# Attention and a gated FFN in one kernel: loads of w_out in pieces of 64 columns, two of its loads triggered sooner, and q and k of heads 8 to 17 prepared at other ticks

## The chip, the cores and the metric

The kernel runs on one core of one Trainium2 chip. The time is the device time of one launch in microseconds (us). A core has five engines: TensorE (PE, with its weight loads shown apart as PEld), VectorE (DVE), ScalarE (ACT), GpSimd (POOL) and SyncE (SP), which mostly issues DMAs. Transfers run on 16 DMA engines beside them. Three runs of the kernel before gave 1164.59, 1169.75 and 1159.92 us, so the median is 1164.59 us.

## The reference

```python
# attention: batch 8, heads 8, S = 576, head size 64
scores = q @ k.T / 8
cum  = cumsum(maximum(s, 0))                       # one s per position and head
bias = minimum(-(cum[:, None] - cum[None, :]), 0)
scores = where(causal, -1e9, scores + bias)
attn = exp(scores - max); attn = attn / (sum + 1e-9)
x = (attn @ v), heads side by side                 # 4608 rows x 512
# gated FFN, the weights are float64 in HBM
gate = 1 / (1 + exp(-(x @ w_gate)))                # w_gate, w_val: 512 x 1536
out  = (gate * (x @ w_val)) @ w_out                # w_out: 1536 x 512
```

q, k, v and s are float32, and so is the output.

## The kernel before, in words

**Heads and ticks.** There are 64 heads (8 batches of 8). Each has 5 query tiles, and the main loop counts a tick n for each tile of each head, n = 5*i + t for head i and tile step t. Heads go in pairs p = i // 2, with j = i % 2. Heads 0 to 7 run in float32 (functions that begin with n_; tiles such as s7, na_ps, nt_ps, nx_ps). From head 8 on, q and k are split into a high and a low float16 half, and the work is done in three float16 products.

**One head from 8 on.** load_qk (L338) fetches q and k of a pair; qk_square and qk_scale find a power of two to scale them by; split_qk (L378) makes the halves by two ACT copies (L386, L388) and two DVE operations (L387, L389) and issues one DMA transpose on SP's queue (L394), which writes two thirds of the tile T. swap_k (L398) then copies two halves of T into its last third by two SBUF-to-SBUF DMAs, also on SP's queue (L399, L400). T has two buffers. For each tile, s_part multiplies T with the first third (L445) and then with the last (L446), so the first product needs the transpose and the second needs the swap. max_part (L470, L473) adds the bias from the row rl (L454), takes the minimum and the exponential on DVE and ACT; p_part splits the probabilities (L477, L482) and transposes them by DMA on SP's queue (L493) into pt; av_part (L505 to L507) multiplies with v. load_crow (L405) brings the row of cumulated s of the next head into one of two buffers, again on SP's queue.

**Weights.** The three weights come as pairs of int32, are decoded on DVE (L271 to L273) and split into float16 high and low (L291 on ACT, L292 on DVE). There are 18 steps. Steps 0 to 11 take one block of 128 columns of w_gate and w_val each; steps 12 to 17 take 256 rows of w_out each, 1 MB in float64, by two DMAs of 512 KB on ACT's queue (L251 and L258). The room for raw weights is shared: `outroom` lists for each w_out step which raw buffer it uses, which one for decoding, and after which step its load may start. weight_step decodes one step and triggers the loads that its step sets free.

**FFN.** From tick 44 on, three FFN units per tick are put between the heads until the first two g are through: unit (g, f) takes 256 rows of x and one of 12 blocks of the hidden size. ffn_in (L656) gives the tile gv, ffn_mid the split hidden tile h, ffn_out (L686) the product of h with w2[f], 512 columns of w_out as the moving operand, into o. The first two g wait for their ffn_out until w_out is there.

**What sets the order.** A scheduler with a model of the engines' times picks, per engine, among the steps that the ticks have made ready; `first()` gives a block a high priority, and `pin` or keep_in_program_order holds an instruction at its place. A moved step can so move others on all engines. Each engine then carries out its list in order.

The lines that change most around the heads are:

```python
if j == 0 and t == 4 and i + 2 >= NN:   # NN = 8
    qk_square(p + 1)
if NN - 1 <= i and j == 1:
    if t == 0:
        qk_scale(p + 1)
    if t == 1:
        split_qk(i + 1)
if t == 3 and NN - 1 <= i:
    swap_k(i + 1)
```

Of the kernel before, what the change touches and what calls it, by code (L numbers as in the profile page):

```python
# [7 lines left out]
F16 = mybir.dt.float16  # L8
F32 = mybir.dt.float32
F32R = mybir.dt.float32r  # L10
I32 = mybir.dt.int32
# [5 lines left out]
P = 128  # L17
# [6 lines left out]
def tile_attention_then_gated_ffn(  # L24
# [13 lines left out]
    NT, DM = out.shape  # L38
    DFF = w_gate.shape[1]
    NH = B * H  # L40
    NPAIR = H // 2
    NC = DM // P
    NF = DFF // P
# [4 lines left out]
    NTL = len(TILES)  # L48
# [4 lines left out]
    NN = H  # L53
# [3 lines left out]
    cp = ctx.enter_context(tc.tile_pool(name="cp", bufs=1))  # L57
# [10 lines left out]


    w1 = [cp.tile([P, NC, 2, 2, P], F16, name=f"w1_{f}") for f in range(NF)]  # L70
    w2all = cp.tile([P, NF, 2, DM], F16, name="w2all")
    w2 = [w2all[:, f] for f in range(NF)]
    e_s = [cp.tile([P, n * P], F32, name=f"e_{i}") for i, (_, _, n) in enumerate(SETS)]
    p_s = [cp.tile([P, 2, n * P], F16, name=f"p16_{i}") for i, (_, _, n) in enumerate(SETS)]

# [128 lines left out]
    spare = {}  # L204
# [6 lines left out]

    raw0 = lp.tile([P, 8 * P, 2], I32, name="ws0")
    dec0 = lp.tile([P, 8 * P], I32, name="wa0")
    flat = w2all.rearrange("p f l n -> p (f l n)").bitcast(I32)
    raw = [raw0] + [flat[:, i * 16 * P : (i + 1) * 16 * P].rearrange("p (n t) -> p n t", t=2) for i in range(2)]
    dec = [dec0] + [flat[:, i * 8 * P : (i + 1) * 8 * P] for i in range(4, 6)]

# [3 lines left out]

    for i in (1, 2):
        raw.append(t2big[:, 8 * i * GT : 8 * (i + 1) * GT].bitcast(I32).rearrange("p (n t) -> p n t", t=2))
    outroom = [(4, 0, 0), (5, 0, 0), (0, 0, NF - 3), (3, 0, NF - 1), (0, 0, NF + 2), (0, 0, NF + 4)]

    def room(n):

# [6 lines left out]
    def load_weight(n):  # L234
        o, f = wsteps[n]
        fs = slice(f * P, (f + 1) * P)
        r, d, _ = room(n)
        for x, src in enumerate((w_out,) if o else (w_gate, w_val)):
            src = src[f * P : (f + 2) * P, :] if o else src[:, fs]
            if wide:  # L240
                src = src.bitcast(I32)
                dst = r.rearrange("p n t -> p (n t)")
            else:
                dst = d.bitcast(F32)
            if o == 0:
                src = src.rearrange("(c p) n -> p c n", p=P)
                dst = dst.rearrange("p (c x n) -> p c x n", c=NC, x=2)[:, :, x]
            else:
                src = src.rearrange("(x p) (h n) -> h p x n", p=P, h=2)
                dst = dst.rearrange("p (x h n) -> h p x n", x=2, h=2)  # L250
                ins = nc.scalar.dma_start(dst[0], src[0])  # L251
                if n < NF + 2:
                    tc.keep_in_program_order(ins)
                src, dst = src[1], dst[1]
            if n < 2:
                nc.sync.dma_start(dst, src)
            else:
                ins = nc.scalar.dma_start(dst, src)  # L258
                if n == 2 or NF <= n < NF + 2:
                    tc.keep_in_program_order(ins)  # L260

    def decode_weight(n):

        o, f = wsteps[n]
        r, a, _ = room(n)
        if not wide:
            return a.bitcast(F32)
        m = w2all[:, f : f + 2].rearrange("p f l n -> p (f l n)") if o else w1[f].rearrange("p c g l n -> p (c g l n)")
        m = m.bitcast(I32)
        nc.scalar.activation(a.bitcast(F32), r[:, :, 1].bitcast(F32), AF.Copy, scale=2.0 ** -112)  # L270
        nc.vector.tensor_scalar(m, a, 3, 0x7FFFFFF8, ALU.logical_shift_left, ALU.bitwise_and)  # L271
        nc.vector.scalar_tensor_tensor(a, a, -0x80000000, m, ALU.bitwise_and, ALU.bitwise_or)
        nc.vector.scalar_tensor_tensor(a, r[:, :, 0], 29, a, ALU.logical_shift_right, ALU.bitwise_or)  # L273
        return a.bitcast(F32)

    def split_weight(n, a):

        o, f = wsteps[n]
        if o:
            a = a.rearrange("p (x n) -> p x n", x=2)  # L280
            hi, lo = w2all[:, f : f + 2, 0], w2all[:, f : f + 2, 1]
        else:
            a = a.rearrange("p (c n) -> p c n", n=P)
            hi, lo = (w1[f].rearrange("p c g l n -> p (c g) l n")[:, :, l] for l in range(2))
        ss = wp.tile([P, 1], F32, tag="wss", name=f"wss{n}")
        nc.scalar.activation(hi, a, AF.Square, accum_out=ss)
        tot = wp.tile([P, 1], F32, tag="wst", name=f"wtot{n}")
        nc.gpsimd.partition_all_reduce(tot, ss, P, ADD_REDUCE)
        pow2_of(wscale[:, o, f : f + 1 + o], tot, f"w{n}")
        sc = wscale[:, o, f : f + 1]  # L290
        nc.scalar.activation(hi, a, AF.Copy, scale=sc)  # L291
        nc.vector.scalar_tensor_tensor(lo, a, sc, hi, ALU.mult, ALU.subtract)  # L292
# [43 lines left out]
    qk32, qkc, T, crow, v32, v16, vx, PT, xq, S_ps, rl, AV = {}, {}, {}, {}, {}, {}, {}, {}, {}, {}, {}, {}  # L336
# [14 lines left out]
    def qk_square(p):  # L351
        t = qk32[p]
        ss = ssq[p % 2]
        for i in range(2):
            junk = wp.tile([QP, 2 * QC * D], F16, tag="jq", name=f"jq{p}_{i}", bufs=1)
            pin(nc.scalar.activation(junk, t[:, i].rearrange("p h c d -> p (h c d)"), AF.Square,
                                     accum_out=ss[:QP, i : i + 1]))
        tot = wp.tile([P, 2], F32, tag="qkt", name=f"qkt{p}")
        nc.gpsimd.partition_all_reduce(tot, ss, P, ADD_REDUCE)
        qkc[p] = tot  # L360
# [353 lines left out]
    for wnext["load"] in range(2):  # L714
        load_weight(wnext["load"])
# [13 lines left out]
    for n in range(nticks + 12):  # L729
        if n == NTL * EARLY:  # L730
            more_room()
        i, t = divmod(n, NTL)
# [10 lines left out]
        if 2 <= n < nticks + 2:  # L743
            a, z = divmod(n - 2, NTL)
# [5 lines left out]
        if 1 <= n < nticks + 1:  # L750
            a, z = divmod(n - 1, NTL)
# [7 lines left out]
        if 3 <= n < 3 + NTL * NN:  # L759
            with first():  # L760
                a, z = divmod(n - 3, NTL)
# [11 lines left out]
        if i < NH:  # L773
            p, j = divmod(i, 2)
            b, h = divmod(i, H)
# [4 lines left out]
            if i + 2 < NN:  # L780
                if j == 0 and t == 1:
                    n_load(p + 1)
                    load_v(p + 1)
                if j == 1 and t == 2:
                    with first():
                        n_prep(p + 1)
            elif j == 0 and t == 2 and i + 2 < NH:
                if p + 1 not in qk32:
                    load_qk(p + 1)
                if i < NN:  # L790
                    load_v(p + 1)
            if NN <= i and i + 1 < NH and j == 1 and t == 2:
                load_v(p + 1)
            if NN <= i and j == 0 and t == 0:
                split_v(p)
            if not spare:
                if j == 0 and t == 4 and i + 2 >= NN:
                    qk_square(p + 1)
                if NN <= i and j == 0 and t == 1:
                    split_qk(i + 1)  # L800
                if NN - 1 <= i and j == 1:
                    if t == 0:
                        qk_scale(p + 1)
                    if t == 1:
                        split_qk(i + 1)
                if t == 3 and NN - 1 <= i:
                    swap_k(i + 1)
            elif i <= EARLY + 1:
                if j == 0:
# [46 lines left out]
            elif b == 1:  # L856
                if VSQ <= n < VSQ + vch:
                    v_square(2, n - VSQ)
                if VSQ + 5 <= n < VSQ + 5 + vch:
                    c = VSQ + 4 + vch - n  # L860
# [15 lines left out]
        if n >= NE and state["u"] < 2 * NF:  # L876
            fdone = min(NF, int((n - NE + 1) * FPT))
            while state["u"] < 2 * fdone:
                f = state["u"]
# [17 lines left out]
        m = n - (11 if n > 2 * NTL * H + 30 else 7)  # L897
# [40 lines left out]
```

## Time and profile before

| | |
|---|---|
| median of three runs | 1164.59 us |
| profiled execution, its own time | 1161.21 us |
| its span | 1159.4 us, 30337 instructions |
| granted TensorE clock, mean | 0.979 |
| busy in the span | PE 1095.0, DVE 775.0, ACT 749.2, POOL 264.9 us |
| DMA | 157.62 MB, mean 136 GB/s |

The profiled execution took 1.8 us more than its span. TensorE is busy for 94% of the span; the gaps lie in the first third. The page's slices are 29 us each. In the answers by window, each engine has its busy time and, in brackets, the number of its instructions; then come the granted clock as a share of full speed, the busy share of the DMA engines and the GB/s. In a timeline a row begins with the start and the duration in us, and brackets at its end hold the idle time before the instruction and what ended it. SPq and ACTq rows are the issues of DMAs. In the groups by line, the last numbers are busy us in all and mean ns of one instruction.

### The profile page before, as it was taken

How to read it: one execution, taken by the hardware profiler on the slowest of the kernel's cores; microseconds unless marked ns; L12 is line 12 of the kernel's file. 1: busy time of each engine (PE TensorE's matmuls, PEld its weight loads, DVE VectorE, ACT ScalarE, POOL GpSimd, SP SyncE). 2: the span in 40 equal slices, each digit the busy share in tenths (PEclk: the TensorE clock that was granted, in tenths of full speed). 3: DMA queues.
4: the chain of work that ended last, by engine and by line, in shares of the span. 5: the costliest groups of instructions: out<-in, count | busy, mean ns of one | idle time of the engine just before them, and what ended most of it. 6: DMA issues, size and time to landing. Idle time of an engine off the chain costs nothing.

```text
span 1159.4 us, 30337 instructions
## 1 busy us (share of the span) xinstructions
PE 1095.0 (94%) x11644; PEld 855.9 (74%) x11644; DVE 775.0 (67%) x2393; ACT 749.2 (65%) x1465; POOL 264.9 (23%) x570
## 2 busy tenths in 40 slices
PE   6786789989999999999999999999999999999997
PEld 5664677656777887778777777778877887787775
DVE  6888879785788777776566577777777775222221
ACT  6988667776777877676656577667777764233222
POOL 5535333231222222121111122222222221000000
PEclk9879899999999999999999999999999999999999
DMA  9675678898889797886737578877877764000000
GB/s 276 199 223 141 129 152 167 177 186 160 154 164 193 151 187 157 153 160 115 164 66 150 99 159 167 168 152 164 154 160 145 146 122 88 12 20 19 1 19 19
DMA packets 435886, 157.62 MB, mean 136 GB/s; under 512 B 403551, under 2 KB 423007, under 8 KB 435742
## 3 DMA queue, kind: packets, MB, share of 16 engines
q1 hardware_dynamic: 418398, 127.12, 57.1%
q10 hardware_dynamic: 13824, 16.78, 4.6%
q0 software_dynamic: 3520, 11.80, 3.1%
q8 instruction: 91, 1.49, 0.5%
q14 instruction: 53, 0.43, 0.1%
HBM read 56.92 MB, written 9.58 MB: 57 GB/s over the span
## 4 chain that ended last, share of the span: by engine, by line
PE 60%; issue 23%; DMA 5%; DVE 4%; ACT 3%; POOL 3%; SPq 1%; ACTq 0%; POOLq 0%; DVEq 0%
PE gv L656 33%; PE o L686 16%; PE s L446 3%; PE s L445 3%; DMA pt<-p 1%; PE av L505 1%; PE av L507 1%; PE av L506 1%; DMA T<-T 1%; POOL rl L460 1%; DMA T<-qk 1%; POOL cr L460 1%; PE na_ps L604 1%; DVE e L470 1%; DMA nqk<-in_q_dram 1%
## 5 line engine op out<-in xcount | busy, mean ns | idle before, releaser
L656 PE MATMUL gv<-x,w 128*128 128x256 f16 (+3 forms) x6912 | 614.9, 247 | 3.9 <-DVE t2f L663 2.3
L656 PEld LDWEIGHTS <-w 128*128 128x128 f16 x6912 | 535.1, 98 | 61.4 <-issue 4.6
L686 PE MATMUL o<-w2all,h 128*128 128x512 f16 x1296 | 314.8, 379 | 0.0
L460 POOL TENSOR_SCALAR_AFFINE_SELECT rl<-rl 128x64 f32<-128x64 f32 (+1 forms) x280 | 113.7, 407 | 512.0 <-DVE em L470 453.3
L473 ACT ACTIVATE e<-e,em 128x576 f32<-128x576 f32 x280 | 154.4, 554 | 88.0 <-DVE em L470 85.9
L661 ACT ACTIVATE th<-gv,scb 128x256 f32<-128x256 f32 (+3 forms) x288 | 111.3, 411 | 147.5 <-PE gv L656 142.5
L686 PEld LDWEIGHTS <-h 128*128 128x128 f16 x1296 | 123.4, 98 | 106.4
L663 DVE SCALAR_TENSOR_TENSOR t<-th,gv 128x256 f32<-128x256 f32 x192 | 80.0, 417 | 133.1 <-ACT th L661 131.9
L470 DVE CUSTOM_DVE_ANT_0 e<-s,rl,qkcf 128x288 f32<-128x288 f32 x280 | 135.7, 485 | 32.1 <-PE s L446 27.8
L671 ACT ACTIVATE h<-t,hsc 128x256 f16<-128x256 f32 x192 | 96.6, 503 | 80.4 <-DVE t L663 80.3
L482 DVE SCALAR_TENSOR_TENSOR p<-e,p 128x384 f16<-128x384 f32 x224 | 102.6, 498 | 41.0 <-ACT p L477 40.2
L672 DVE SCALAR_TENSOR_TENSOR h<-t,hsc,h 128x256 f16<-128x256 f32 x192 | 93.3, 486 | 43.4 <-ACT h L671 42.6
L477 ACT ACTIVATE p<-e 128x1152 f16<-128x1152 f32 x112 | 112.0, 1000 | 2.5
L505 PE MATMUL av<-v,pt 128*128 128x65 f16 x560 | 67.8, 193 | 5.3 <-DMA pt<-p 5.3
L446 PE MATMUL s<-T 128*128 128x288 f16 (+2 forms) x246 | 62.1, 279 | 11.3 <-DMA T<-T 11.3
L445 PE MATMUL s<-T 128*128 128x288 f16 (+2 forms) x246 | 64.4, 279 | 7.1 <-DMA T<-qk 4.2
L694 POOL DMA_DIRECT2D out_dram<-osb x36 | 20.4, 566 | 211.5 <-ACT osb L693 210.9
L507 PE MATMUL av<-v,pt 128*128 128x65 f16 x560 | 67.8, 194 | 0.0
L506 PE MATMUL av<-v,pt 128*128 128x64 f16 x560 | 67.7, 192 | 0.0
L505 PEld LDWEIGHTS <-pt 128*128 128x128 f16 x560 | 52.5, 98 | 11.0 <-DMA pt<-p 6.1
L408 POOL PARTITION_BROADCAST cr<-cr x63 | 58.5, 929 | 2.1 <-DMA cr<-cum_d 2.0
L506 PEld LDWEIGHTS <-pt 128*128 128x128 f16 x560 | 52.5, 97 | 4.9
(155 smaller groups left out, 1415.0 us busy)
## 6 DMA issues: line engine op xcount, KB each, us to landing
out_dram<-osb POOLq DMA_DIRECT2D x36, 256.0 KB, 2.8
v<-v SPq DMA_DIRECT2D x56, 162.5 KB
v<-in_v_dram SPq DMA_DIRECT2D x64, 128.0 KB
T<-T SPq DMA_DIRECT2D x82, 72.0 KB
t2f<-in_v_dram SPq DMA_DIRECT2D x20, 288.0 KB
qk<-in_q_dram SPq DMA_DIRECT2D x17, 288.0 KB
qk<-in_k_dram SPq DMA_DIRECT2D x17, 288.0 KB
w2all<-in_moe_w_gate_dram ACTq DMA_DIRECT2D x7, 512.0 KB
```

The costliest lines, as they stand in the source:

```text
L445: nc.tensor.matmul(ps[:, : b_ - a], lhs, T[i][:, 0, a:b_], start=True, stop=False)
L446: nc.tensor.matmul(ps[:, : b_ - a], lhs, T[i][:, 2, a:b_], start=False, stop=True)
L460: nc.gpsimd.affine_select(rl[i][:, q0:w], rl[i][:, q0:w], pattern=[[-1, m]], compare_op=ALU.is_ge, fill=-MASKED if i < NN else MASKED, bas ...
L470: nc.vector.tensor_tensor_reduce(e_t[t][:, a:b_], ps[:, : b_ - a], rl[i][:, a:b_], c, init, ALU.add, ALU.min, acc)
L473: nc.scalar.activation(e_t[t][:, :w], e_t[t][:, :w], AF.Exp, bias=init, scale=-1.0)
L477: nc.scalar.activation(p_s[h_][:, 0], e_s[h_], AF.Copy, scale=PSCALE)
L482: nc.vector.scalar_tensor_tensor(flat[:, LOW[t] * P : (LOW[t] + t) * P], e_t[t][:, : t * P], PSCALE, flat[:, kb * P : (kb + t) * P], ALU.m ...
L505: nc.tensor.matmul(AV[i][:, t], hi, v_[:, D : 2 * D + 1], start=kb == 0, stop=False)
L506: nc.tensor.matmul(AV[i][:, t, 0:D], hi, v_[:, 0:D], start=False, stop=False)
L656: nc.tensor.matmul(ps[:, gv, a:e], w1[f][:, cc, gv, wl], x_of(b, cc)[:, xl, c0 + a : c0 + e], start=(c == 0), stop=(c == 3 * NC - 1))
L661: nc.scalar.activation(th[:, a:e], ps[:, 0, a:e], AF.Tanh, scale=scb[b][:, f : f + 1])
L686: nc.tensor.matmul(ps[:m], h[:, hl, tt * P : tt * P + m], w2[f][:, wl], start=(f == 0 and c == 0), stop=(f == NF - 1 and c == 2))
```

## The change

**Layout of w_out.** w2all, the split w_out, was `[P, 12, 2, 512]` (block f, high or low, columns). It is now `[P, 6, 2, 8, 2, 64]`: a pair of blocks, high or low, eight groups of 64 columns, which block of the pair, and the 64 columns. The two halves of one block's row are no longer next to each other: w2[f] is eight runs of 64 columns with a gap of 64 between them. Each load of 512 KB was a half of the columns of 256 rows, in pieces of 256 columns (2 KB in float64); it is now 128 rows with all columns, in pieces of 64 columns (512 B). What split_weight writes, high and low, is now one run of 1024 each; before it was two runs of 512.

**Rooms.** The fifth w_out step (16) now uses the raw buffer of the second one (13) and has the mark `NF + 1`: its load is triggered in weight_step of step 14 (before: of step 15). The sixth (17) takes the room ws0 with the mark `NF + 2`: its load is triggered in step 15 (before: in step 17).

**Ticks.** In the part of the loop for heads 7 to 17, load_qk goes from t = 2 to t = 0 or 1, qk_square from t = 4 to t = 2 or 3, qk_scale from t = 0 of the next head to t = 3 or 4, split_qk from t = 1 to t = 0 (for head 8 to tick 34), and swap_k from t = 3 to t = 2 (for head 8 to tick 36).

```diff
--- before.py
+++ after.py
@@ -68,8 +68,9 @@
 
 
     w1 = [cp.tile([P, NC, 2, 2, P], F16, name=f"w1_{f}") for f in range(NF)]
-    w2all = cp.tile([P, NF, 2, DM], F16, name="w2all")
-    w2 = [w2all[:, f] for f in range(NF)]
+
+    w2all = cp.tile([P, NF // 2, 2, 8, 2, DM // 8], F16, name="w2all")
+    w2 = [w2all[:, f // 2, :, :, f % 2] for f in range(NF)]
     e_s = [cp.tile([P, n * P], F32, name=f"e_{i}") for i, (_, _, n) in enumerate(SETS)]
     p_s = [cp.tile([P, 2, n * P], F16, name=f"p16_{i}") for i, (_, _, n) in enumerate(SETS)]
 
@@ -211,7 +212,7 @@
 
     raw0 = lp.tile([P, 8 * P, 2], I32, name="ws0")
     dec0 = lp.tile([P, 8 * P], I32, name="wa0")
-    flat = w2all.rearrange("p f l n -> p (f l n)").bitcast(I32)
+    flat = w2all.rearrange("p f l h x n -> p (f l h x n)").bitcast(I32)
     raw = [raw0] + [flat[:, i * 16 * P : (i + 1) * 16 * P].rearrange("p (n t) -> p n t", t=2) for i in range(2)]
     dec = [dec0] + [flat[:, i * 8 * P : (i + 1) * 8 * P] for i in range(4, 6)]
 
@@ -221,7 +222,7 @@
 
     for i in (1, 2):
         raw.append(t2big[:, 8 * i * GT : 8 * (i + 1) * GT].bitcast(I32).rearrange("p (n t) -> p n t", t=2))
-    outroom = [(4, 0, 0), (5, 0, 0), (0, 0, NF - 3), (3, 0, NF - 1), (0, 0, NF + 2), (0, 0, NF + 4)]
+    outroom = [(4, 0, 0), (5, 0, 0), (0, 0, NF - 3), (3, 0, NF - 1), (5, 0, NF + 1), (0, 0, NF + 2)]
 
     def room(n):
 
@@ -246,8 +247,9 @@
                 src = src.rearrange("(c p) n -> p c n", p=P)
                 dst = dst.rearrange("p (c x n) -> p c x n", c=NC, x=2)[:, :, x]
             else:
-                src = src.rearrange("(x p) (h n) -> h p x n", p=P, h=2)
-                dst = dst.rearrange("p (x h n) -> h p x n", x=2, h=2)
+
+                src = src.rearrange("(x p) (h n) -> x p h n", p=P, h=8)
+                dst = dst.rearrange("p (h x n) -> x p h n", x=2, h=8)
                 ins = nc.scalar.dma_start(dst[0], src[0])
                 if n < NF + 2:
                     tc.keep_in_program_order(ins)
@@ -265,7 +267,7 @@
         r, a, _ = room(n)
         if not wide:
             return a.bitcast(F32)
-        m = w2all[:, f : f + 2].rearrange("p f l n -> p (f l n)") if o else w1[f].rearrange("p c g l n -> p (c g l n)")
+        m = w2all[:, f // 2].rearrange("p l h x n -> p (l h x n)") if o else w1[f].rearrange("p c g l n -> p (c g l n)")
         m = m.bitcast(I32)
         nc.scalar.activation(a.bitcast(F32), r[:, :, 1].bitcast(F32), AF.Copy, scale=2.0 ** -112)
         nc.vector.tensor_scalar(m, a, 3, 0x7FFFFFF8, ALU.logical_shift_left, ALU.bitwise_and)
@@ -277,8 +279,7 @@
 
         o, f = wsteps[n]
         if o:
-            a = a.rearrange("p (x n) -> p x n", x=2)
-            hi, lo = w2all[:, f : f + 2, 0], w2all[:, f : f + 2, 1]
+            hi, lo = (w2all[:, f // 2, l].rearrange("p h x n -> p (h x n)") for l in range(2))
         else:
             a = a.rearrange("p (c n) -> p c n", n=P)
             hi, lo = (w1[f].rearrange("p c g l n -> p (c g) l n")[:, :, l] for l in range(2))
@@ -784,26 +785,25 @@
                 if j == 1 and t == 2:
                     with first():
                         n_prep(p + 1)
-            elif j == 0 and t == 2 and i + 2 < NH:
-                if p + 1 not in qk32:
+            elif j == 0 and i + 2 < NH:
+                if t == (2 if spare else 1 if i >= NN else 0) and p + 1 not in qk32:
                     load_qk(p + 1)
-                if i < NN:
+                if t == 2 and i < NN:
                     load_v(p + 1)
             if NN <= i and i + 1 < NH and j == 1 and t == 2:
                 load_v(p + 1)
             if NN <= i and j == 0 and t == 0:
                 split_v(p)
             if not spare:
-                if j == 0 and t == 4 and i + 2 >= NN:
-                    qk_square(p + 1)
-                if NN <= i and j == 0 and t == 1:
-                    split_qk(i + 1)
-                if NN - 1 <= i and j == 1:
-                    if t == 0:
+                late = i >= NN
+                if i + 2 >= NN and j == 0:
+                    if t == 2 + late:
+                        qk_square(p + 1)
+                    if t == 3 + late:
                         qk_scale(p + 1)
-                    if t == 1:
-                        split_qk(i + 1)
-                if t == 3 and NN - 1 <= i:
+                if n == NTL * (NN - 1) - 1 or NN <= i and t == 0:
+                    split_qk(max(i + 1, NN))
+                if n == NTL * (NN - 1) + 1 or NN <= i and t == 2:
                     swap_k(i + 1)
             elif i <= EARLY + 1:
                 if j == 0:
```

The order of the instructions differs on DVE between about its rows 166 and 726 of 2392, on ACT between 132 and 440 of 1393; the set of instructions is the same. Line numbers of the changed kernel are one or two higher than before.

The first place is DVE around the split of head 8 (qk16_8; em7 are the maxima of head 7, v16_4 the split v of heads 8 and 9, w1_11 and w2all weights). Before, the split stands among the first maxima of head 7:

```order
L583 ISA e_1_80,em7_4_0_1147<-s7_4_0_1109,cr7_978 128x288
...
L387 SCALAR_TENSOR_TENSOR qk16_8_1152<-qk32_4_1039,qksc4_1131,qk16_8_1152 96x6x64
L389 SCALAR_TENSOR_TENSOR qk16_8_1152<-qk32_4_1039,qksc4_1131,qk16_8_1152 96x6x64
...
L583 ISA e_1_80,em7_4_1_1149<-s7_4_288_1111,cr7_978,em7_4_0_1147 128x288
...
L583 ISA e_1_80,em7_3_0_1169<-s7_3_0_1137,cr7_978 128x448
...
L292 SCALAR_TENSOR_TENSOR w1_11_77<-w2all_78,wscale_111,w1_11_77 128x8x128
L583 ISA e_0_79,em7_2_0_1195<-s7_2_0_1159,cr7_978 128x320
...
L430 SCALAR_TENSOR_TENSOR v16_4_1242<-v32_4_1042,vsc1_1002,v16_4_1242 128x10x64
L583 ISA e_0_79,em7_1_0_1210<-s7_1_0_1180,cr7_978 128x192
...
L583 ISA e_0_79,em7_0_0_1234<-s7_0_0_1200,cr7_978 64x64
...
L292 SCALAR_TENSOR_TENSOR w2all_78<-wa0_137,wscale_111,w2all_78 128x2x512
```

In the changed kernel the same place reads:

```order
L431 SCALAR_TENSOR_TENSOR v16_4_1242<-v32_4_1042,vsc1_1005,v16_4_1242 128x10x64
...
L584 ISA e_1_80,em7_3_0_1171<-s7_3_0_1144,cr7_978 128x448
...
L293 SCALAR_TENSOR_TENSOR w1_11_77<-w2all_78,wscale_111,w1_11_77 128x8x128
L584 ISA e_0_79,em7_2_0_1197<-s7_2_0_1161,cr7_978 128x320
...
L388 SCALAR_TENSOR_TENSOR qk16_8_1121<-qk32_4_981,qksc4_1092,qk16_8_1121 96x6x64
L390 SCALAR_TENSOR_TENSOR qk16_8_1121<-qk32_4_981,qksc4_1092,qk16_8_1121 96x6x64
L584 ISA e_0_79,em7_1_0_1210<-s7_1_0_1182,cr7_978 128x192
...
L293 SCALAR_TENSOR_TENSOR w2all_78<-wa0_137,wscale_111,w2all_78 128x1024
L632 SCALAR_TENSOR_TENSOR x2_132<-nx_ps_2_0_1031,vsc0_327,x2_132 128x320
L584 ISA e_0_79,em7_0_0_1234<-s7_0_0_1200,cr7_978 64x64
...
L615 TENSOR_TENSOR nx3_1180<-na_ps_6_1111,ner6_1177 128x5x64
```

The split of head 8 has gone behind four pieces of work (the split of v, two maxima of head 7 and the split of w1_11) that followed it before.

The second place is SP's queue from the transposes of heads 8 and 9 on (T8, T9; v32_4 is the swapped v, cr9 and cr10 the rows of cumulated s). Before:

```order
L405 DMA cr9_1240<-cum_d_114 1x576
L394 DMA_TRANSPOSE T8_1157<-qk16_8_1152 128x12x96
L399 DMA T8_1157<-T8_1157 64x576
L400 DMA T8_1157<-T8_1157 64x576
L435 DMA v32_4_1042<-v16_4_1242 64x1300 x2
L405 DMA cr10_1407<-cum_d_114 1x576
L394 DMA_TRANSPOSE T9_1269<-qk16_9_1264 128x12x96
```

In the changed kernel:

```order
L436 DMA v32_4_1042<-v16_4_1242 64x1300
L395 DMA_TRANSPOSE T8_1126<-qk16_8_1121 128x12x96
L406 DMA cr10_1419<-cum_d_114 1x576
L400 DMA T8_1126<-T8_1126 64x576
L401 DMA T8_1126<-T8_1126 64x576
L395 DMA_TRANSPOSE T9_1253<-qk16_9_1248 128x12x96
```

The row cr10 now stands ahead of the swap of T8, and the two copies of v ahead of its transpose.

The third place is PE at head 8's first scores (s8), with the rest of heads 6 and 7 (na_ps, nt_ps, nx_ps) and the first FFN unit (gv0_0). Before:

```order
L446 MATMUL s8_3_0_1248<-T8_1157 128x448
L604 MATMUL na_ps_6_1093<-v32_3_747,p16_0_81 128x65
L595 MATMUL nt_ps_7_3_3_1182<-ident_88,e_1_80 128x128
...
L595 MATMUL nt_ps_7_3_0_1187<-ident_88,e_1_80 128x128 x3
L628 MATMUL nx_ps_2_3_1034<-ident_88,nx2_895 128x128 x2
```

In the changed kernel:

```order
L596 MATMUL nt_ps_7_3_0_1189<-ident_88,e_1_80 128x128 x3
L629 MATMUL nx_ps_2_3_1037<-ident_88,nx2_895 128x128 x2
...
L446 MATMUL s8_3_0_1255<-T8_1126 128x448
...
L605 MATMUL na_ps_7_1213<-v32_3_747,p16_1_82 128x65 x4
L596 MATMUL nt_ps_7_0_0_1258<-ident_88,e_0_79 128x128 x3
...
L447 MATMUL s8_3_0_1255<-T8_1126 128x448
...
L657 MATMUL gv0_0_1349<-x0_130,w1_0_66 128x256
```

The transposes and the products of heads 6 and 7 have moved ahead of the products that need T8's swap; they stood behind them.

## Prediction

> **What bounds the kernel now.** I read the page first: TensorE is the engine with most work, and it is idle only in the first third.
>
> ```profile
> PE 1095.0 (94%) x11644; PEld 855.9 (74%) x11644; DVE 775.0 (67%) x2393; ACT 749.2 (65%) x1465; POOL 264.9 (23%) x570
> PE   6786789989999999999999999999999999999997
> ```
>
> Then the busy time by window, which narrows that down (window, length, then PE, PEld, DVE, ACT, POOL busy, the granted clock, the DMA share and GB/s):
>
> ```profile
> 100.00:360.00 260.00, 226.64 (x2425) 175.50 (x2425) 205.76 (x646) 188.98 (x366) 75.19 (x145) 0.97 0.81 160
> 111.00:123.00 12.00, 5.19 (x29) 4.35 (x29) 4.97 (x16) 5.86 (x13) 0.86 (x3) 0.72 0.92 214
> 123.00:140.00 17.00, 13.56 (x100) 10.34 (x99) 16.82 (x54) 16.09 (x30) 9.11 (x14) 0.90 0.40 78
> 145.00:156.00 11.00, 7.12 (x88) 6.26 (x87) 8.23 (x23) 7.34 (x11) 3.54 (x6) 0.99 0.96 221
> 400.00:420.00 20.00, 20.00 (x310) 16.55 (x308) 13.27 (x40) 14.97 (x32) 6.67 (x15) 1.00 0.84 178
> ```
>
> From 400 us on TensorE has no gap, so there a change of the other engines' order is worth nothing. Between 100 and 360 us it is idle for 260 - 226.64 = 33.4 us, and that is all that can be won by timing. The stretch from 111 to 123 is the worst: PE, DVE and ACT are each busy for less than half of it and the clock falls to 0.72, while the DMA engines work at 0.92. From 123 to 140 DVE is the bound, with 16.82 of 17 us. From 145 to 156 the DMA engines are full again.
>
> Who is waited for, by the waits of PE (total, times, longest):
>
> ```profile
> PE s L446 <- DMA T<-T: 11.3, 6, 6.7
> PE av L505 <- DMA pt<-p: 5.3, 4, 3.9
> PE s L445 <- DMA T<-qk: 4.2, 5, 1.9
> ```
>
> The longest of them, in the timeline (start, duration, engine, and in brackets the idle time before):
>
> ```profile
> 104.68 0.61 DVE L387 SCALAR_TENSOR_TENSOR qk<-qk,qksc,qk 96x384 f16<-96x384 f32 x1
> 105.21 0.61 DVE L389 SCALAR_TENSOR_TENSOR qk<-qk,qksc,qk 96x384 f16<-96x384 f32 x1
> 105.84 1.41 SPq L394 DMA_TRANSPOSE T<-qk  x1
> 109.59 0.88 DVE L430 SCALAR_TENSOR_TENSOR v<-v,vsc,v 128x640 f16<-128x640 f32 x1
> 110.65 0.36 DVE L583 CUSTOM_DVE_ANT_0 e<-s,cr 128x192 f32<-128x192 f32 x1 [0.18 <-POOL cr L460]
> 110.74 0.53 SPq L399 DMA_DIRECT2D T<-T  x1
> 110.81 0.39 ACTq L251 DMA_DIRECT2D w2all<-in_moe_w_out_dram  x1
> 111.36 0.22 DVE L583 CUSTOM_DVE_ANT_0 e<-s,cr 64x64 f32<-64x64 f32 x1 [0.34 <-POOL cr L460]
> 111.51 1.27 DVE L292 SCALAR_TENSOR_TENSOR w2all<-wa,wscale,w2all 128x1024 f16<-128x1024 f32 x1
> 113.77 0.54 DVE L631 SCALAR_TENSOR_TENSOR x<-nx_ps,vsc,x 128x320 f16<-128x320 f32 x1
> 117.76 0.42 PE L446 MATMUL s<-T 128*128 128x288 f16 x1 [6.70 <-DMA T<-T]
> 120.83 0.17 DVE L610 TENSOR_SCALAR ner<-na_ps 128x5 f32<-128x5 f32 x1 [6.53 <-PE na_ps L604]
> ```
>
> Head 8 is the first that needs T. Its split ends at 105.82, the transpose is issued at 105.84, the swap can start 4.9 us later (110.74), and its result is there at 117.76, 7.0 us after its issue, because a w_out load of 1 MB was issued at 110.81. Behind the waiting product on PE stands the end of heads 6 and 7 (na_ps), and DVE is idle for 6.53 us for want of it. What DVE could have done in that time then comes in the stretch where DVE is full.
>
> **Head 8, its split and its wait.** By its name the change makes the split sooner, but the order has it later on DVE, behind v16_4, the split of w1_11 and two more maxima of head 7. The last of that set to run before is the v row, which ends at 109.59 + 0.88 = 110.47. DVE has no gap worth the name from 104 to there, so the changed split ends when the same set is done, about 110.5. The transpose takes 4.9 us as now; the nearest rows for it run from 3.46 (a T transpose) to 9.63 (a pt transpose beside a load), by the chain of waits (start, share of the chain in us):
>
> ```profile
> 137.80 3.46 DMA T<-qk
> 145.90 9.63 DMA pt<-p
> 239.89 2.86 DMA T<-T
> 246.54 3.15 DMA T<-T
> ```
>
> That gives 115.4 for the issue of the swap. cr10, now ahead of the swap on SP's queue, waits for head 7's last maximum, which is the fourth DVE step behind the split: 0.36 + 1.27 + 0.54 + 0.22 = 2.4 us by the rows at 110.65, 111.51, 113.77 and 111.36. That is inside the 4.9 us, and it costs something only if the transpose lands in less than 2.4. The two v copies that now stand ahead of the transpose are ready at 110.5 as well; their issue is not in the sum, the late end holds it. The swap takes 2.9 to 3.15 us without a load beside it and 7.0 with one. The load of step 15 is still issued near 110.8, so its 3.6 us of transfers (worked out below) are nearly over by 115.4; I take 3.5. The second products would then start at 118.9, 1.1 us later than now (ends: 110.5 + 3.46 + 2.86 = 116.8, 0.9 sooner; 110.5 + 9.63 + 3.0 = 123.1, 5.4 later).
>
> Against this stands what is no longer behind the wait. In the changed PE order the end of heads 6 and 7 comes ahead of the second products, and with it these DVE steps can be done before 118.9, in the idle 6.53 us:
>
> ```profile
> 122.22 0.49 DVE L614 TENSOR_TENSOR nx<-na_ps,ner 128x320 f32<-128x320 f32 x1
> 122.62 0.68 DVE L271 TENSOR_SCALAR w2all<-wa 128x1024 int32<-128x1024 int32 x1
> 123.83 1.22 DVE L272 SCALAR_TENSOR_TENSOR wa<-wa,w2all 128x1024 int32<-128x1024 int32 x1
> 124.96 0.48 DVE L631 SCALAR_TENSOR_TENSOR x<-nx_ps,vsc,x 128x256 f16<-128x256 f32 x1
> 126.25 1.22 DVE L273 SCALAR_TENSOR_TENSOR wa<-t2f,wa 128x1024 int32<-128x1024 int32 x1
> ```
>
> That is 0.49 + 0.68 + 1.22 + 0.48 + 1.22 = 4.1 us out of a stretch in which DVE is the bound. So 4.1 - 1.1 = **3.0 us gained** (ends -1.3 and +5.0). What is late next is DVE itself in 123 to 140.
>
> **The pt wait at 152.** The load of step 16 is issued half a microsecond behind the transpose of pt:
>
> ```profile
> 145.90 1.74 SPq L493 DMA_TRANSPOSE pt<-p  x1
> 146.39 0.37 ACTq L251 DMA_DIRECT2D ws<-in_moe_w_out_dram  x1
> 155.57 0.20 PE L505 MATMUL av<-v,pt 128*128 128x65 f16 x1 [3.88 <-DMA pt<-p]
> ```
>
> The transpose's 9.63 us end in a wait of 3.88. In the changed ACT order this load stands right behind the square of step 13, near 120 us, and step 17's near 130, in or just ahead of the stretch with a DMA share of 0.40. With a landing of 4.9 the pt is there before it is asked for. The load of q and k stays beside it, so I take **3.5 us gained** (ends 0 and 3.9).
>
> **The other T and pt waits.** Without the two long ones there are 11.3 - 6.7, 5.3 - 3.9 and 4.2, in all 10.2 us, spread from 130 to 360. Splits and swaps one tick sooner should take some; but the scheduler can place them behind other work, as it did for head 8, and only heads up to 17 change. I take a quarter, **2.5 us gained** (ends 6 us, and -1.4, the small pt waits doubled, since loads now come sooner).
>
> **The smaller pieces.** Each w_out load has four times as many packets. Rows of the DMA groups in three windows that hold pieces of 2 KB, 1 KB and 256 B in turn (window, in the text: 92 to 104, 20 to 34, 60 to 80 us; packets, MB, share of 16 engines):
>
> ```profile
> q10 hardware_dynamic: 545, 1.05, 25.1%
> q10 hardware_dynamic: 2915, 2.89, 63.9%
> q1 hardware_dynamic: 3459, 0.86, 19.4%
> ```
>
> Share times window times 16 over packets is 88.4, 49.1 and 17.9 ns per packet. On the line between the last two, 512 B takes 28.3 ns. A load is 512 packets now, 512/16 x 88.4 = 2.8 us; it becomes 2048/16 x 28.3 = 3.6 us, 0.8 more (ends: nothing, and 3.5 if a piece cost what a 1 KB one does, 128 x 49.1 = 6.3). Six loads are 4.8 us of DMA time, most of it hidden by TensorE's work; but loads 16 and 17 now lie beside T9's transpose and swap and pt of head 8, on which PE does wait. I take **1.5 us lost** (ends 0 and 4).
> [...]
>
> **What costs nothing.** split_weight writes one run of 1024 in place of two of 512. The ACT rows of the two forms that exist differ by 7 ns, and six such steps are nothing:
>
> ```profile
> L291 ACT ACTIVATE w<-w2all,wscale 128x1024 f16<-128x1024 f32 x8 | 9.1, 1143 | 0.8 <-DVE ner L611 0.7
> L291 ACT ACTIVATE w2all<-wa,wscale 128x1024 f16<-128x1024 f32 x6 | 6.8, 1136 | 0.0
> L686 PE MATMUL o<-w2all,h 128*128 128x512 f16 x1296 | 314.8, 379 | 0.0
> ```
>
> The row of L686 is in rival C.
>
> **The sum.** 3.0 + 3.5 + 2.5 - 1.5 = 7.5 us less. The profiled execution took 1161.21 us, so 1153.7; it lies 3.4 us below the median of 1164.59, which goes to **1157**. All ends on one side give -1.3 + 0 - 1.4 - 4 = -6.7, a median of 1171, and 5.0 + 3.9 + 6.0 - 0 = 14.9, a median of 1150.
>
> **Rivals.**
> *A: the waits go for good.* Every term comes out near its upper end: T8 is there early, DVE's work is done in its old gap, and the loads run where the DMA share is 0.40. For it speaks that all of it lies in the 33.4 us of gaps and that the clock of 0.72 would come back as well. Against it: the split of head 8 is later in the order. Time 1150.
> *B: the change does not do what it says and the wait only moves.* T8's split is behind v16_4, its transpose behind two v copies, and T9's transpose and swap now meet load 16 near 120. If T8's swap lands at the late end (-1.3), and what pt gains at 152 (3.5) is given back by T9's swap, which then takes 7.0 in place of 3.0 us, the sum is about nothing. For it speaks the row at 110.81: a load beside a swap has cost 4 us. Time 1164, up to 1168 with the smaller pieces at their price.
> *C: w2[f] in eight runs slows the products of ffn_out.* They read 512 columns in one run now, and in eight after. The L291 rows are the nearest: output in eight runs of 128 takes 7 ns more than in two of 512, 1.2 ns for each further run. Seven further runs would be 8.2 ns on each of 1296 products, 10.6 us, all on PE's path, since from 400 on PE never waits: 1157 + 10.6 = 1168, slower than before. It decides from 7.5 us / 1296 = 5.8 ns per product. Against it, 7 ns on one row of eight instructions is hardly more than noise, and no row shows PE with a cut moving operand.
> [...]
>
> **Chances.** Forecast 0.48 (gains of 3 to 11.6, 1153 to 1162), A 0.22, B 0.20, C 0.10. The three runs differ by 10 us, so less than 1% (11.6 us: below 1153 or above 1176) can hardly be told from no change. Faster by over 1%: A and the edge of the forecast, 0.24. Slower by over 1%: C at a larger price or B with every end against it, 0.07. Within 1%: 0.69. The range goes from 1147, A less what the runs scatter, to 1169, which holds B and most of C; the forecast's own is 1153 to 1162.
>
> **What would show it.** Right: the wait for T8's swap ends near 119 with the na_ps products of head 7 ahead of it; DVE has no idle 6.5 us there; no pt wait between 145 and 160; w_out loads issued near 110, 120 and 130; 100 to 360 us holds about 7 us less idle PE. The packets of a w_out load take 28 ns. Wrong: a mean of ffn_out's products above 379 ns (C); a wait of 4 us or more for T9 (B); or a new wait for DVE between 123 and 150, which would say that the 4.1 us were not what held PE.

## The result and the profile after

The changed kernel took 1151.86 us (median of 4 runs, 1150.75 to 1152.65) against 1167.17 for the kernel before in the same comparison: a ratio of 0.9876, with a 95% interval of 0.9835 to 0.9917. Timed again later with 12 runs beside other kernels it gave 1155.25 us against 1163.27, a ratio of 0.9928 (0.9898 to 0.9957). So the gain is 8 to 15 us by the medians (5 to 19 by the ends of the intervals), and the first figure of 15 rests on four runs of each kernel. The forecast was 7.5. Both medians lie in the stated range of 1147 to 1169 us; in the forecast's own range of 1153 to 1162 lies only the second.

The page after shows the same work in a shorter span (1149.0 us in place of 1159.4):

```profile
PE 1093.9 (95%) x11644; PEld 856.3 (75%) x11644; DVE 774.6 (67%) x2393; ACT 748.6 (65%) x1465; POOL 261.9 (23%) x570
PE   6787889989999999999999999999999999999997
```

The windows of the changed kernel, in the columns of the prediction:

```profile
100.00:360.00 260.00, 236.66 (x2523) 184.20 (x2523) 214.46 (x685) 196.89 (x380) 75.38 (x151) 0.97 0.82 168
111.00:123.00 12.00, 11.19 (x75) 9.90 (x73) 9.15 (x22) 8.31 (x16) 2.72 (x6) 0.72 0.72 170
123.00:140.00 17.00, 12.56 (x110) 9.26 (x108) 16.03 (x50) 13.80 (x24) 6.34 (x12) 0.80 1.01 223
140.00:160.00 20.00, 18.18 (x202) 15.79 (x199) 17.63 (x44) 14.38 (x26) 5.65 (x10) 1.00 0.66 134
160.00:360.00 200.00, 185.76 (x2087) 142.18 (x2086) 160.84 (x534) 149.41 (x295) 54.32 (x113) 1.00 0.85 171
```

Two windows of the kernel before that the prediction did not show:

```profile
140.00:160.00 20.00, 14.81 (x177) 12.66 (x178) 14.40 (x41) 10.89 (x20) 4.08 (x9) 0.91 0.81 180
160.00:360.00 200.00, 184.07 (x2059) 140.71 (x2056) 159.01 (x508) 146.31 (x289) 55.00 (x111) 1.00 0.85 168
```

Idle PE between 100 and 360 us fell from 33.4 to 23.3 us, by 10.0, which is the 10.4 us of the span but for a few tenths. By stretch: 111 to 140 from 10.25 to 5.25 (6.81 + 3.44 before, 0.81 + 4.44 after), 140 to 160 from 5.19 to 1.82, 160 to 360 from 15.93 to 14.24. The clock in 111 to 123 is 0.72 as before, though PE is now busy there nearly all the time.

The waits of PE in the changed kernel:

```profile
PE av L506 <- DMA pt<-p: 5.3, 5, 2.0
PE s L446 <- DMA T<-qk: 3.8, 3, 2.3
PE s L447 <- DMA T<-T: 1.6, 2, 0.9
```

The wait for the swap of T fell from 11.3 to 1.6 us. The waits for pt are 5.3 in all as before, only in shorter pieces and at another place. From 160 to 360 us they were, before and then after:

```profile
PE av L505 <- DMA pt<-p: 1.4, 3, 1.0
PE av L506 <- DMA pt<-p: 4.8, 3, 2.0
```

Head 8 in the timeline of the changed kernel:

```profile
108.35 0.55 ACTq L253 DMA_DIRECT2D w2all<-in_moe_w_out_dram  x1
109.45 0.64 DVE L390 SCALAR_TENSOR_TENSOR qk<-qk,qksc,qk 96x384 f16<-96x384 f32 x1
110.11 2.14 SPq L395 DMA_TRANSPOSE T<-qk  x1
115.64 0.49 SPq L400 DMA_DIRECT2D T<-T  x1
115.67 1.04 PE L446 MATMUL s<-T 128*128 128x288 f16 x3
116.51 1.80 PE L605 MATMUL na_ps<-v,p 128*128 128x65 f32 x8
116.83 1.21 DVE L275 SCALAR_TENSOR_TENSOR wa<-t2f,wa 128x1024 int32<-128x1024 int32 x1
118.75 0.82 PE L605 MATMUL na_ps<-v,p 128*128 128x65 f32 x6
119.40 0.60 PE L447 MATMUL s<-T 128*128 128x288 f16 x3
```

The split ends at 110.09 and the swap is issued at 115.64, 5 us later than in the kernel before. Yet the second products (L447) show no wait: while the swap travels, PE does the products of heads 6 and 7, and DVE decodes.

### The profile page after: what moved, and what is told of

Same layout as the page of the kernel before. It is cut to its first block, busy times and chain, and to the rows that moved or that the text cites. A ratio compares the mean times of both kernels' runs of the same rounds, so it can differ in the third digit from the quotient of the medians.

```text
span 1149.0 us, 30327 instructions
## 1 busy us (share of the span) xinstructions
PE 1093.9 (95%) x11644; PEld 856.3 (75%) x11644; DVE 774.6 (67%) x2393; ACT 748.6 (65%) x1465; POOL 261.9 (23%) x570
## 4 chain that ended last, share of the span: by engine, by line
PE 51%; issue 25%; DMA 6%; DVE 5%; ACT 3%; POOL 2%; SPq 1%; POOLq 0%; ACTq 0%; DVEq 0%
PE gv L657 28%; PE o L687 14%; PE s L447 2%; PE s L446 2%; DMA v<-in_v_dram 2%; DMA qk<-in_q_dram 1%; POOL rl L461 1%; PE av L506 1%; PE av L508 1%; DVE e L471 1%; PE av L507 1%; DMA pt<-p 1%; SPq L420 1%; ACT e L474 1%; PE av L510 1%
## 5 line engine op out<-in xcount | busy, mean ns | idle before, releaser
L461 POOL TENSOR_SCALAR_AFFINE_SELECT rl<-rl 128x64 f32<-128x64 f32 (+1 forms) x280 | 111.3, 398 | 519.6 <-DVE em L471 464.3
L447 PE MATMUL s<-T 128*128 128x288 f16 (+2 forms) x246 | 61.8, 279 | 1.7 <-DMA T<-T 1.6
L506 PEld LDWEIGHTS <-pt 128*128 128x128 f16 x560 | 52.4, 97 | 11.8 <-DMA pt<-p 6.9
L455 DVE TENSOR_SCALAR rl<-cr,qkcf 128x576 f32<-128x576 f32 x56 | 29.1, 519 | 40.0 <-POOL cr L409 39.8
```

What stands on the lines that cost most here:

```text
L461: nc.gpsimd.affine_select(rl[i][:, q0:w], rl[i][:, q0:w], pattern=[[-1, m]], compare_op=ALU.is_ge, fill=-MASKED if i < NN else MASKED, bas ...
L506: nc.tensor.matmul(AV[i][:, t], hi, v_[:, D : 2 * D + 1], start=kb == 0, stop=False)
```

## The experiments

**How they are laid out.** The change has three parts: the shape of w_out (layout and loads), the marks of outroom, and the ticks of q and k. Each was run alone on the kernel before and left out of the changed one. Theory "order": the gain comes from the order of PE and DVE at head 8, and the shape brings that order. Rival "ticks": the sooner q and k make it. Rival "packets": the smaller packets let the other transfers through.

All of them, with the ratio to the kernel before of the same comparison, and from each profile the issue of the loads of steps 15, 16 and 17, the longest wait for T8's swap, all waits for pt, and idle PE between 100 and 360 us:

| kernel | ratio (95%) | loads issued at, us | T8 wait | pt waits | idle PE |
|---|---|---|---|---|---|
| before | 1 | 111, 146, 182 | 6.7 | 5.3 | 33.4 |
| changed | 0.9876 (0.9835 to 0.9917) | 108, 118, 132 | none | 5.3 | 23.3 |
| changed_again | 0.9928 (0.9898 to 0.9957) | 108, 118, 132 | none | 5.9 | 25.1 |
| w_out_shape_only | 0.9941 (0.9916 to 0.9967) | 107, 133, 165 | none | 4.2 | 29.1 |
| rooms_only | 1.0016 (0.9991 to 1.0041) | 113, 130, 149 | 7.2 | 9.3 | 34.1 |
| ticks_only | 0.9992 (0.9969 to 1.0014) | 116, 150, 186 | 3.5 | 5.4 | 27.5 |
| no_shape | 1.0027 (1.0005 to 1.0048) | 110, 127, 148 | 4.3 | 14.3 | 32.2 |
| no_rooms | 0.9914 (0.9883 to 0.9945) | 108, 133, 165 | none | 3.0 | 24.8 |
| no_ticks | 0.9920 (0.9888 to 0.9951) | 108, 118, 132 | none | 7.6 | 24.1 |
| pieces_2kb | 0.9895 (0.9865 to 0.9924) | 109, 118, 132 | none | 5.9 | 22.6 |
| load15_away | 0.9966 (0.9942 to 0.9989) | 143, 159, 178 | 2.4 | 7.2 | 27.9 |
| rows_4kb | 0.9958 (0.9934 to 0.9982) | 100 and 110, 124, 146 | 1.6 | 8.2 | 28.6 |
| loads_late | 0.9996 (0.9972 to 1.0019) | 134, 156, 182 | none | 15.4 | 32.9 |
| loads_spread | 0.9913 (0.9883 to 0.9942) | 123, 138, 169 | none | 10.4 | 23.7 |

(T8 waits under 1 us are told as none. rows_4kb issued its two halves of step 15 apart. The idle time of ticks_only stands beside a lower mean clock, 0.969, so it says less than the others': PE got through 2401 products in that window, against 2425 before and 2523 in the changed kernel.)

In the diffs that follow, only the lines that matter are printed.

**The shape alone.**

```diff
-w2all = cp.tile([P, NF, 2, DM], F16, name="w2all")
+w2all = cp.tile([P, NF // 2, 2, 8, 2, DM // 8], F16, name="w2all")
-src = src.rearrange("(x p) (h n) -> h p x n", p=P, h=2)
+src = src.rearrange("(x p) (h n) -> x p h n", p=P, h=8)
```

> The kernel before with only the new shape of the w_out loads and of w2all. In the order, head 8's split stands behind v16_4 and the end of heads 6 and 7 ahead of the second products, as in the changed kernel; the loads of steps 16 and 17 stay late. Theory 'order' (the gain at head 8 is the order of PE and DVE there, and the load shape brings it): the wait for T8's swap is gone (6.7 to under 1 us), idle PE of 111 to 140 falls by about 5 us, the pt wait near 152 stays; 5 to 7 us less than before. Rival 'ticks' (q and k sooner make the gain): no gain, within 2 us of before.

It gave 1158.26 against 1163.88 us. Its window from 111 to 140 us:

```profile
111.00:140.00 29.00, 24.36 (x183) 19.87 (x183) 25.08 (x71) 22.37 (x41) 6.82 (x16) 0.82 0.73 152
```

4.6 us idle there for 10.25 before: this part alone brings the whole of head 8's gain, as "order" said. The pt wait near 152, which should have stayed, went as well (the longest is 1.6): with this order the load of step 16 goes out at 133 with the old marks too.

**The marks alone.**

```diff
-(0, 0, NF + 2), (0, 0, NF + 4)]
+(5, 0, NF + 1), (0, 0, NF + 2)]
```

> The kernel before with only the two new marks of outroom. Head 8 is ordered as before, so its wait of 6.7 us stays by every theory. The load of step 16 leaves the pt transpose at 146: if it made that wait, the 3.9 us are gone and the time is 3 to 4 us less; if another transfer made it (the load of q and k at 148), the wait stays and the time is within 1.5 us of before.

1166.32 against 1163.88 us, no gain, and not for the reason given. The load of step 16 did leave the transpose (130 us), but step 17 took its place. The timeline of this kernel:

```profile
148.60 0.37 ACTq L251 DMA_DIRECT2D ws<-in_moe_w_out_dram  x1
148.66 1.88 SPq L493 DMA_TRANSPOSE pt<-p  x1
150.59 0.64 SPq L346 DMA_DIRECT2D qk<-in_q_dram  x1
160.42 0.23 PE L505 MATMUL av<-v,pt 128*128 128x65 f16 x1 [7.33 <-DMA pt<-p]
```

A load 0.06 us ahead of the transpose of pt, and a wait of 7.33 us. The loads of q and k, the other candidate, lie there too. But in the changed kernel they also follow a transpose of pt (148.13, then 150.92 and 151.74), with no w_out load near, and no wait for pt falls between 140 and 160. So the w_out load is the likelier cause, though no run moves it alone, and the marks alone don't clear the place.

**The ticks alone.**

```diff
-if j == 0 and t == 4 and i + 2 >= NN:
-    qk_square(p + 1)
+if i + 2 >= NN and j == 0:
+    if t == 2 + late:
+        qk_square(p + 1)
...
-if t == 3 and NN - 1 <= i:
+if n == NTL * (NN - 1) + 1 or NN <= i and t == 2:
     swap_k(i + 1)
```

> The kernel before with only the new ticks of q and k. Theory 'order': head 8 keeps the old order on PE (second products ahead of the end of heads 6 and 7), so the wait of about 6.7 us stays; the later heads' waits give 0 to 3 us. Rival 'ticks': 6 us or more less than before.

1163.32 against 1163.88 us: no gain that can be told from noise (the interval reaches from 3.6 us less to 1.6 more), where the rival "ticks" needed 6. It falls. The T8 wait did not stay at 6.7, as expected, but fell to 3.5: the load went out 0.5 us behind the swap, which took 5.2 us from issue to use (115.65 to 120.83).

**The changed kernel with one part left out.** The three are the diffs above, taken back one at a time.

> The changed kernel with the old shape of the w_out loads and of w2all (new marks and new ticks stay). In the order, head 8 is as in the kernel before. Theory 'order': the wait for T8's swap is back (5 to 7 us), and the kernel is 4 to 7 us slower than the changed one. Rival 'ticks': within 2 us of the changed kernel.

> The changed kernel with the old marks of outroom. Head 8 is as in the changed kernel. If the load of step 16 made the pt wait near 152, a wait of 2 to 4 us for pt or T comes back there and the kernel is 2 to 4 us slower than the changed one; if not, within 1.5 us of it.

> The changed kernel with the old ticks of q and k. Theory 'order': head 8 is as in the changed kernel, so it stays within 2 us of it, perhaps 1 to 2 us slower by the waits of heads 9 to 17. Rival 'ticks': most of the gain is lost, 5 us or more slower than the changed one.

Without the shape the kernel took 1169.13 us against 1166.48 of before, and lost everything; that is 12 to 18 us more than the changed kernel by the ratios, where 4 to 7 were expected. Its T8 wait was 4.3 (5 to 7 expected), and its pt waits were 14.3 us. Most of these, 9.6, fall between 160 and 360 us, behind its last w_out load (148 us), so no w_out load beside them explains them:

```profile
PE av L505 <- DMA pt<-p: 9.6, 9, 2.7
```

Without the marks it took 1155.82, without the ticks 1156.55. In no_rooms the loads of 16 and 17 are at 133 and 165 us. A transpose of pt follows each of them by 0.9 to 1.0 us (133.80 and 165.46), and yet no wait for T or pt over 1.8 us came back; my 2 to 4 us did not come. On top of the shape, marks and ticks may give something between them (the ratio goes from 0.9941 to 0.9928 or 0.9876, 1.5 to 7.6 us), but the intervals overlap, the kernel with either left out is no slower than the changed one in its second timing (0.9914 and 0.9920 against 0.9928), and these runs don't settle it.

**The packets.** The changed kernel with pieces of 2 KB; each engine's instructions stand in the same order as in the changed kernel, so only the packets differ.

```diff
-w2all = cp.tile([P, NF // 2, 2, 8, 2, DM // 8], F16, name="w2all")
+w2all = cp.tile([P, NF // 2, 2, 2, 2, DM // 2], F16, name="w2all")
-src = src.rearrange("(x p) (h n) -> x p h n", p=P, h=8)
+src = src.rearrange("(x p) (h n) -> x p h n", p=P, h=2)
```

> The changed kernel with pieces of 256 columns (2 KB) in place of 64 (512 B): each engine's instructions are in the same order as in the changed kernel, only the packets are larger (and w2[f] is two runs). Theory 'order': within 1.5 us of the changed kernel; by the prediction's price of the small pieces 1 to 2 us faster. Rival 'packets' (small packets let the swaps and transposes through): 3 us or more slower, with T8's swap taking over 5 us from issue to the second products.

1153.88 us, a ratio of 0.9895, between the two of the changed kernel: "packets" falls. Since the order is the same, the two profiles give the price of a packet directly. The w_out queue between 108 and 116 us, first with 2 KB, then with 512 B:

```profile
q10 hardware_dynamic: 544, 1.05, 38.4%
```

```profile
q10 hardware_dynamic: 2080, 1.05, 47.3%
```

Share times 8 us times 16 over packets is 90.4 ns and 29.1 ns. A load is 512/16 x 90.4 = 2.89 us and 2048/16 x 29.1 = 3.73 us, 0.84 us more.

**The load beside the swap.** The kernel before with the load of step 15 behind the decoding of step 14. PE and DVE keep their order around head 8.

```diff
-(3, 0, NF - 1), (0, 0, NF + 2), (0, 0, NF + 4)]
+(0, 0, NF + 2), (0, 0, NF + 3), (0, 0, NF + 4)]
```

> The kernel before with the load of step 15 put into the room ws0 behind step 14's decoding, so that it is issued near 145 us in place of 110.8; 16 and 17 follow in the same room. PE and DVE are ordered as before around head 8. If the load beside the swap makes the 7.0 us of the swap, the wait of 6.7 us falls to about 2.7 and idle PE of 111 to 123 falls by 4 us; if the swap is slow by itself, the wait stays over 5 us. The later loads may cost up to 3 us near 145 to 200, so the time is 1 to 4 us less.

The timeline of this kernel:

```profile
106.79 1.41 SPq L394 DMA_TRANSPOSE T<-qk  x1
111.72 0.53 SPq L399 DMA_DIRECT2D T<-T  x1
114.42 0.42 PE L446 MATMUL s<-T 128*128 128x288 f16 x1 [2.37 <-DMA T<-T]
```

The swap takes 2.7 us from issue to use, against 7.0 with the load beside it (110.74 to 117.76), and the wait falls from 6.7 to 2.4, as expected. The kernel is 3.9 us faster by its medians (1.3 to 6.8 by the interval). So the collision was most of the wait at head 8 (4.3 of 6.7 us), and the order is a second way to be rid of it: in the changed kernel PE has other work for the 3.8 us from the swap's issue to its use (115.64 to 119.40).

**Whole rows.** The changed kernel with w_out loaded in rows of 4 KB (the layout keeps a block's 512 columns together, the marks and ticks stay). By the order, the second products of head 8 stand ahead of most of head 7's end again.

```diff
-src = src.rearrange("(x p) (h n) -> x p h n", p=P, h=8)
+src = src.rearrange("(x p) n -> x p n", p=P)
```

> The changed kernel with w_out loaded in whole rows (pieces of 512 columns, 4 KB, w2[f] in one run); new marks and new ticks stay. By the order alone head 8 is near the kernel before again: second products of head 8 ahead of most of the end of head 7. Theory 'order': a wait of 2 to 6 us for T8's swap is back, and the gain is mostly lost, 1160 to 1168 us. Rival 'pieces' (the layout or the larger or smaller pieces themselves give the gain): within 3 us of the changed kernel or faster.

1158.60 against 1163.27 us: about half of the gain, and a T8 wait of 1.6 us, below the 2 to 6 expected, since half of the load went out at 99.92 and no longer met the swap. It was faster than "order" allowed and slower than "pieces" did.

**Where the loads go, with the good order.**

```diff
-(3, 0, NF - 1), (5, 0, NF + 1), (0, 0, NF + 2)]
+(0, 0, NF + 2), (0, 0, NF + 3), (0, 0, NF + 4)]   # loads_late
+(5, 0, NF + 1), (0, 0, NF + 2), (0, 0, NF + 4)]   # loads_spread
```

> The changed kernel with the loads of steps 15, 16 and 17 one after the other in the room ws0: none near T8's or T9's swap (110 to 127 us), all between 130 and 200. The end of heads 6 and 7 stays ahead of the second products. Theory 'order': with that order the load beside the swap has no price, so head 8 gains nothing by it; T9's wait of 2.3 us goes, pt waits come back near 145 to 200; within 3 us of the changed kernel. Rival 'collision' (what the changed kernel won is the load's place): 2 us or more faster.

> The changed kernel with the loads of steps 15, 16 and 17 issued near 119, 132 and 165 us in place of 108, 118 and 132. T8's transpose has no load beside it, T9's swap has. Theory 'order': within 2 us of the changed kernel. If the spread takes the load from the stretch of 123 to 140 where the DMA share is 1.0, 1 to 3 us faster, and this beats both kernels.

> The changed kernel itself, beside the three others on one chip: it has four runs so far, and the parts are compared with it. Every theory expects a ratio of 0.985 to 0.992 to before.

(changed_again gave 0.9928, a little above the 0.985 to 0.992 that every theory expected.) loads_late took 1164.28 us against 1163.27: the whole gain is gone, although the end of heads 6 and 7 stays ahead of head 8's second products and no wait for the swap shows. Here "order" as I had put it falls. The waits of PE for pt in this kernel, and the place of the longest:

```profile
PE av L506 <- DMA pt<-p: 15.4, 6, 5.2
```

```profile
155.72 0.55 ACTq L253 DMA_DIRECT2D ws<-in_moe_w_out_dram  x1
155.93 1.87 SPq L494 DMA_TRANSPOSE pt<-p  x1
164.68 0.23 PE L506 MATMUL av<-v,pt 128*128 128x65 f16 x1 [5.16 <-DMA pt<-p]
```

The pt waits are 15.4 us where the changed kernel has 5.3. Of them 7.6 end at two products (138.58 and 164.68 us) behind transposes that went out within 1.2 us of a load. Another 6.1 (2.5 at 178.92, 3.6 behind 200 us) have no w_out load near them. And the marks changed the order again: the split of head 9 now goes ahead of the last decoding step (115.34 and 115.87; in the changed kernel 117.97 and 116.83). From 111 to 140 us most of the idle time of before is back (8.8 us of 10.25; 5.25 in the changed kernel), and its longest wait is for a maximum on DVE:

```profile
111.00:140.00 29.00, 20.24 (x143) 16.68 (x143) 22.88 (x64) 19.23 (x36) 6.70 (x13) 0.77 0.51 107
135.75 0.30 PE L446 MATMUL s<-T 128*128 128x320 f16 x1 [3.27 <-DVE em L471]
```

So this run does not show what the place of the loads costs by itself. loads_spread, with the first two loads at 123 and 138, has 10.4 us of pt waits and still 1155.93 us; it is neither faster nor slower than the changed kernel in the same comparison (0.9913 against 0.9928).

**What follows.** That the shape makes the gain is shown from both sides: it gains alone, and without it nothing is left. It is not the size of the packets (pieces_2kb). How it does so is in part argued. A theory that fits the long waits: a w_out load delays the small SBUF transfer that it lies beside (a swap of T took 7.0 us with one and 2.7 without), and PE pays where that transfer is next in its order. At head 8 the shape's order puts the end of heads 6 and 7 in between, so that PE pays nothing; and with that order the loads of steps 16 and 17 go out sooner and miss the transpose of pt near 146. The kernels without that order (before, rooms_only, ticks_only, no_shape) have T8 waits of 3.5 to 7.2 us and no gain clear of noise; load15_away and rows_4kb, where the load misses the swap by its place, in whole or in part, gain about half.

What does not follow from the theory are the pt waits behind 160 us in no_shape and loads_late, with no w_out load near; why those two lose everything stays open. So does why the scheduler's model of the engines answers to this shape: the orders of the kernels with pieces of 2 KB and 512 B are the same, and that of whole rows is nearly the old one. No run has the new order with the old shape, so the order has not been tried by itself.

## Why the prediction was right, and where it was not

**The time and the sign** held: 7.5 us less was forecast, 8.0 and 15.3 were measured by the two pairs of medians, 10.5 by the two profiled executions (1161.21 and 1150.75). That the sum came so near is in part luck: counted over the waits, the term of head 8 was 2 us or more too small and that of the other waits about as much too large. The chances leaned to "within 1%", and the two ratios, 1.2% and 0.7% faster, lie on both sides of that bound.

**Head 8 (3.0 us, measured 5.0 of idle PE in 111 to 140).** The chain held almost to the tenth: split at 110.5 (110.09), swap issued at 115.4 (115.64), second products at 118.9 (119.40). The transpose took 5.5 us rather than 4.9. The load issued at 108.35 lay beside it, and with no load there it took 3.6 (110.09 to 113.67 in loads_late); but in the kernel before it took 4.9 with no w_out load beside it, so the load is not shown to be the whole cause. The term was mis-sized in one step: I took the later swap off the gain, 1.1 us, as if PE stood still for it. There was work for PE until 119.40, so lateness cost nothing. All five DVE steps that I counted ended by 118.04, and DVE's busy time in 111 to 123 rose by 4.2 us (4.97 to 9.15), for the 4.1 counted. Without the 1.1 taken off the term is 4.1, and the other 0.9 us is not accounted for. My upper end was 5.0 as well, but for a swap that starts sooner, and that did not happen. Nor did the gain show where I looked for it: from 123 to 140 DVE is still busy for 16.03 of 17 us and idle PE rose from 3.44 to 4.44; all of it lies in 111 to 123.

**The pt wait at 152 (3.5 us, measured 3.4 in 140 to 160).** That wait went, as forecast, and the load of step 16 went out near 120, as read from the order on ACT. What the prediction did not ask is which part of the change sends it there. rooms_only shows that the marks alone put step 17 in its place and nearly double the wait, and w_out_shape_only that the shape's order alone moves the load to 133.

**The other waits (2.5 us, measured 1.7 in 160 to 360).** The quarter was a choice, and counted as the prediction counted it, over the waits for T and pt without the two long ones, it did not come: 10.2 us before, 10.7 after (1.6 + 5.3 + 3.8). The swaps fell, from 4.6 to 1.6, but the waits for pt rose from 1.4 to 5.3. The two long waits that went, 6.7 and 3.9 us, make 10.6, as much as the whole fall of idle time (10.0). The ticks, to which I gave this term, show no gain by themselves.

**The smaller pieces (1.5 us lost).** The price was right: 29.1 ns a packet against 28.3, and 0.84 us a load against 0.8. A load took 29% longer than with 2 KB (3.73 against 2.89 us). Whether 1.5 us of it reach the time is open: idle PE with 2 KB is 0.7 to 2.4 us less than in the two profiles of the changed kernel, but the intervals of the times overlap.

**The rivals.** A came nearest in the first comparison (1151.86 against its 1150), though its ground, that the loads run where the DMA share is low, was not the ground: the share in 123 to 140 rose from 0.40 to 1.01, and the clock of 0.72 in 111 to 123, which was to come back, stayed. B showed in one place: T9's transpose and swap met the load of step 16 at 118.24 and PE waited 2.3 us at 125.40 for T9's transpose; not the 4 us that it needed. C fell; the products of ffn_out read eight runs in the time of one, 379 ns each as before:

```profile
L687 PE MATMUL o<-w2all,h 128*128 128x512 f16 x1296 | 314.8, 379 | 0.0
```

**What the reasoning missed** is which part does it. The sum was made from the order of the whole, and the price came out; but it did not ask what makes that order, put only a loss on the shape and gave a term to the ticks. The runs give most of the gain to the shape: 5.6 us alone, and none without it.

## What to carry to other kernels

When a scheduler sets the order, read the new order and price that: the part of a change that moves the time can be one that, by its words, is only a layout. Here a load of 1 MB cost a small transfer that it lay beside 2.5 to 4.8 us (a swap of 5.2 to 7.5 in place of 2.7), so look for what PE does next after each of them: either move the load, or put other work of PE in between. At head 8 PE did not pay for a late swap (issued 4.9 us later than before) once it had work ahead of the products that need it.

## What the hardware showed that I had not expected

A swap of T (two copies of 72 KB) took 2.7 us from issue to use with no load beside it, and 7.0 and 7.5 us (112.80 to 120.28 in rooms_only) with a 1 MB load issued within 0.1 us of it; with the load 0.2 and 0.5 us behind, it took 5.2 (109.98 to 115.13 in no_shape, 115.65 to 120.83 in ticks_only). The row for rooms_only:

```profile
112.80 0.53 SPq L399 DMA_DIRECT2D T<-T  x1
112.87 0.40 ACTq L251 DMA_DIRECT2D w2all<-in_moe_w_out_dram  x1
120.28 0.42 PE L446 MATMUL s<-T 128*128 128x288 f16 x1 [7.16 <-DMA T<-T]
```

The products of ffn_out, 512 columns each, took 379 ns with the moving operand in eight runs of 128 bytes, as they did with it in one run.
